# A float64-weight MLP pair behind attention: four conversion operations in two parts, low weights on VectorE, second activation read from its bank

## The chip, the cores and the metric

The kernel runs on one core of one Trainium2 chip. The metric is the device time of one launch in microseconds (us). Engines are named as in the profile: PE is TensorE (matmul), PEld its weight load, DVE is VectorE, ACT is ScalarE, POOL is GpSimd, SP is SyncE, which here only issues DMAs. [...]

## The reference, cut to what matters

```python
def _moe_ref(x, w_in, w_out):            # x 1792x768, w_in 768x2048, w_out 2048x768
    h = x @ w_in
    r = np.maximum(h, 0.0)
    g = r * r
    return (g @ w_out).astype(np.float32)

def _moe2_ref(x, w_in, w_out):
    h = x @ w_in
    relu6 = np.clip(h + 3.0, 0.0, 6.0)
    g = h * relu6 / 6.0
    return (g @ w_out).astype(np.float32)

def reference(**kwargs):
    ...
    attn_out = _attn_ref(**attn_kwargs)  # 4 batches, 12 heads, 448 rows, 64 per head
    ...
    x = _moe_ref(x=x, **moe_kwargs)
    return _moe2_ref(x=x, **moe2_kwargs)
```

The four weight matrices come as float64 (dividing a float32 array by a float64 scalar made them so); everything else is float32.

## The kernel before

Four batches are worked in two groups of two. Each group runs attention and then two MLPs. An MLP has a hidden phase (x @ w_in, then the activation) and a project phase (g @ w_out). Weights come in units of 128x768 numbers: 16 units for each phase, 64 for the two MLPs. A unit feeds 36 matmuls of 448 columns in two halves of 18, one for each batch of the group (e = 0 and 1). In the hidden phase each half sums in a PSUM bank of its own (two banks, tag `bm`), and its activation reads that bank.

Products are made exact enough by splitting: a number is rounded to fp32r (`wh`, `gh`, `xh`), and the remainder is kept beside it (`wl`, `gl`, `xl`); three products are summed. `split(n)` makes `wh` on ACT and `wl` from it; `act` is the activation; `split_g` makes `gh` (on DVE in the first MLP, on ACT in the second) and then `gl` on POOL.

Only group 0 reads the float64 weights: `load(n)` brings a unit as pairs of 32-bit words, `convert(n)` makes float32 of them with integer operations in place, and `store(n)` writes the float32 unit to DRAM, from where group 1 reads it back. So group 1 does the same matmuls with no conversion. All this lies in one tile `arena`: two slots for raw units, three (`wr`) for converted ones.

The order on each engine is the order in which the code is written (the scheduler is off), and each engine works its queue strictly in that order. `run` goes over the units. For unit n it writes: load a later unit; the activation of the second half of unit n-1 (`rest`); `convert(n + 2)`; `split(n + 1)`; `store(n)`; `split_g` of that `rest`; then the 18 matmuls of half 0, their activation and `split_g`, and the 18 matmuls of half 1. While group 0 projects for the second time, steps of group 1's attention stand between the units. At the start, `convert(0)`, `split(0)` and `convert(1)` stand among the last steps of the attention (`opening` and the main loop), beside `xr` copies out of PSUM (L314) and the splits of x.

Of the kernel before, what the change touches and what calls it, by code (L numbers as in the profile page):

```python
# [39 lines left out]

F64_LEAST = 2.0 ** -15
F64_MOST = (2.0 - 2.0 ** -3 - 2.0 ** -23 ) * 2.0 ** 16

# [15 lines left out]
def attention_mlp_kernel(ctx: ExitStack, tc, qT, kT, v, w_pre, w_post, mask, w1_in, w1_out, w2_in, w2_out, outT):  # L59
# [38 lines left out]
    w2f = cst.tile([R, G, RI], F32, name="w2f")  # L98
    three = cst.tile([P, 1], F32, name="three")

# [372 lines left out]
    class Mlps:  # L473
# [26 lines left out]

        def convert(self, n):

            if n >= len(self.units) or self.gi > 0:
                return
            words = self.raw(n).bitcast(U32).rearrange("p (n e) -> p n e", e=2)
            low, high = words[:, :, 0], words[:, :, 1]
            wr = self.wr(n)
            bits = wr.bitcast(U32)
            nc.scalar.activation(wr, high.bitcast(F32), AF.Abs)  # L509
            nc.vector.tensor_scalar(wr, wr, F64_LEAST, F64_MOST, op0=ALU.max, op1=ALU.min)  # L510
            nc.vector.tensor_scalar(  # L511
                bits, bits, 3, 0x7FFFFFFF, op0=ALU.logical_shift_left, op1=ALU.bitwise_and)
            nc.vector.tensor_scalar(  # L513
                high, high, 0x80000000, 0x40000000, op0=ALU.bitwise_and, op1=ALU.bitwise_or)
            nc.vector.scalar_tensor_tensor(  # L515
                out=bits, in0=low, scalar=29, in1=bits, op0=ALU.logical_shift_right, op1=ALU.bitwise_or)
            nc.vector.tensor_tensor(out=bits, in0=bits, in1=high, op=ALU.bitwise_xor)

# [5 lines left out]
        def split(self, n):  # L524
            if n >= len(self.units):
                return
            wh = sh.tile([P, self.W], F32R, tag="wh", name=f"wh{self.gi}_{n}", bufs=2)
            wl = sh.tile([P, self.W], F32R, tag="wl", name=f"wl{self.gi}_{n}", bufs=2)
            nc.scalar.activation(wh, self.wr(n), AF.Copy)  # L529
            nc.gpsimd.tensor_tensor(out=wl, in0=self.wr(n), in1=f(wh), op=ALU.subtract)  # L530
            self.ready[n] = wh, wl
# [12 lines left out]
        def act(self, which, fc, e, hp):  # L544
# [6 lines left out]
            else:  # L551
                a = sh.tile([P, S], F32, tag="w2", name=f"a{nm}", bufs=2)
                nc.scalar.activation(r, hp[:, :S], AF.Relu, bias=three)
                nc.scalar.activation(a, hp[:, :S], AF.Copy, scale=1.0 / 6.0)  # L554
                nc.vector.scalar_tensor_tensor(out=g, in0=r, scalar=6.0, in1=a, op0=ALU.min, op1=ALU.mult)
            return which, fc, e, g
# [58 lines left out]
        def run(self, mp, behind):  # L615

            rest = None
            for n, (kind, which, m, _) in enumerate(self.units):
                self.load(n + (3 if self.gi == 0 else 2))
                if rest:  # L620
                    rest = self.act(*rest)
                if n == 0:
                    self.split(1)
                self.convert(n + 2)
                if n > 0:
                    self.split(n + 1)
                self.store(n)
                if rest:
                    self.split_g(*rest)
                    rest = None  # L630
                wh, wl = self.ready.pop(n)
                if kind == "h":
# [14 lines left out]
                    hp = self.hidden(which, m, 0, wh, wl)  # L647
                    self.split_g(*self.act(which, m, 0, hp))
                    rest = (which, m, 1, self.hidden(which, m, 1, wh, wl))
# [31 lines left out]
    with tc.manual_schedule():  # L681
        nc.vector.memset(three, 3.0)
        warm = sh.tile([P, 1], F32, tag="wh", name="warm", bufs=2)
        nc.scalar.activation(warm, three, AF.Exp)
        att = Attention(0)
# [68 lines left out]
```

## Time and profile before

| | us |
|---|---|
| median of 3 runs | 1480.28 (1479.43 to 1483.08) |
| the profiled execution | 1481.33, of which its span is 1479.5 |
| PE busy | 1407.2 (95% of the span) |
| DVE, ACT, POOL busy | 754.5, 678.3, 718.3 (51%, 46%, 49%) |

The span runs from the first to the last instruction of the profiled execution; 1.83 us of its time lie outside. Shares are means over attention, hidden and project phases of both groups, which have different limits.

### The profile page before, as it was taken

To read this page: it belongs to the slowest core of one execution; us is meant where nothing else is said; L and a number is where in the kernel's file an instruction comes from. 1 tells how busy PE (TensorE), PEld (TensorE's weight loads), DVE (VectorE), ACT (ScalarE), POOL (GpSimd) and SP (SyncE) were. 2 spreads that over 40 slices of the span, in tenths; PEclk is the share of its full clock that TensorE was granted. 3 is DMA by queue.
4 is the path that set the end of the run, shared out by engine and by line. 5 is a ranking of instruction groups with operands and counts; after the bars stand their busy time and mean duration, and the time that the engine had idled before them with its cause. 6 is when DMAs were issued, how large, how long until landed. Compare 5 with 4: busy or idle time off the path is not lost.

```text
span 1479.5 us, 22801 instructions
## 1 busy us (share of the span) xinstructions
PE 1407.2 (95%) x8512; PEld 1253.7 (85%) x8512; DVE 754.5 (51%) x1356; ACT 678.3 (46%) x1293; POOL 718.3 (49%) x662
## 2 busy tenths in 40 slices
PE   8889999999999998889998999999999999999999
PEld 4678888788899987779997888889999999999998
DVE  4877667776777588888756786571110001111000
ACT  4767665444422344444436666664442113554121
POOL 1667766555532255443235677675554223555221
PEclk9999999999999999999999999999999999999999
DMA  5354533445465544447755444431111111111121
GB/s 143 108 142 112 147 102 99 149 131 158 131 198 152 160 129 128 128 128 210 213 176 145 127 119 142 116 103 54 54 54 54 54 54 54 54 54 54 54 91 49
DMA packets 72211, 167.53 MB, mean 113 GB/s; under 512 B 9125, under 2 KB 47525, under 8 KB 72101
## 3 DMA queue, kind: packets, MB, share of 16 engines
q1 hardware_dynamic: 68645, 160.59, 37.4%
q10 hardware_dynamic: 3456, 5.51, 1.0%
q8 instruction: 66, 1.08, 0.3%
q14 instruction: 44, 0.36, 0.1%
HBM read 96.86 MB, written 30.67 MB: 86 GB/s over the span
## 4 chain that ended last, share of the span: by engine, by line
PE 70%; DVE 16%; ACT 4%; issue 4%; POOL 4%; DMA 1%; SPq 0%; POOLq 0%; ACTq 0%; DVEq 0%
PE ps_a L587 21%; PE ps_h L573 16%; PE bs L587 9%; PE ps_o L279 8%; PE ps_x L306 5%; DVE arena L513 5%; DVE arena L515 3%; PE ps_m L231 2%; PE ps_m L233 2%; ACT arena L509 2%; PE bs L193 2%; PE bs L194 2%; PE ps_m L232 2%; DVE arena L510 1%; DVE arena L511 1%
## 5 line engine op out<-in xcount | busy, mean ns | idle before, releaser
L530 POOL TENSOR_TENSOR wl<-arena,wh 128x768 fp32r<-128x768 f32 x128 | 246.7, 1927 | 435.5 <-ACT wh L529 384.6
L224 POOL TENSOR_TENSOR tl<-t,th 120x448 fp32r<-120x448 f32 x165 | 192.5, 1167 | 36.7 <-ACT th L222 30.5
L529 ACT ACTIVATE wh<-arena 128x768 fp32r<-128x768 f32 x128 | 107.8, 842 | 218.7 <-PE bs L587 163.6
L587 PE MATMUL ps_a<-gh,wl 128*128 128x448 f32 x544 | 198.4, 365 | 2.5 <-POOL wl L530 2.5
L587 PE MATMUL ps_a<-gh,wh 128*128 128x448 f32 x544 | 199.4, 367 | 0.0
L279 PEld LDWEIGHTS ps_o<-w2s,p 120*112 120x112 f32 (+1 forms) x1440 | 174.1, 178 | 23.1 <-POOL w2s L268 13.3
L279 PE MATMUL ps_o<-w2s,p 120*112 120x120 f32 (+1 forms) x1440 | 180.6, 269 | 8.0 <-POOL w2s L268 8.0
L573 PE MATMUL ps_h<-yh,wh 128*128 128x448 f32 x384 | 141.7, 369 | 19.4 <-ACT a L554 19.4
L573 PE MATMUL ps_h<-xh,wl 128*128 128x448 f32 x384 | 141.8, 369 | 8.4 <-POOL wl L530 8.4
L573 PE MATMUL ps_h<-xl,wh 128*128 128x448 f32 x384 | 141.1, 367 | 0.9 <-DVE xl L541 0.6
L248 ACT ACTIVATE p<-ps_m,mx 120x448 f32<-120x448 f32 x180 | 113.2, 629 | 60.7 <-PE ps_o L279 28.8
L573 PE MATMUL ps_h<-xh,wh 128*128 128x448 f32 x384 | 140.6, 366 | 0.2 <-ACT r L549 0.2
L573 PE MATMUL ps_h<-yl,wh 128*128 128x448 f32 x384 | 140.7, 367 | 0.0
L573 PE MATMUL ps_h<-yh,wl 128*128 128x448 f32 x384 | 140.2, 365 | 0.0
L565 POOL TENSOR_TENSOR gl<-g,gh 128x448 fp32r<-128x448 f32 x80 | 95.9, 1204 | 78.8 <-ACT gh L564 44.3
L294 DVE COPY a<-ps_o 112x480 f32<-112x480 f32 (+1 forms) x176 | 114.4, 650 | 27.5 <-PE ps_o L279 26.4
L268 POOL TENSOR_SCALAR w2s<-w2f,rz 120x120 f32<-120x120 f32 x180 | 70.3, 390 | 118.7 <-DVE rz L260 102.3
L222 ACT ACTIVATE th<-t 120x448 fp32r<-120x448 f32 x180 | 102.6, 570 | 48.8 <-POOL tl L224 16.4
L587 PE MATMUL ps_a<-gl,wh 128*128 128x448 f32 x340 | 124.2, 365 | 0.0
L240 DVE TENSOR_REDUCE mx<-ps_m 120x1 f32<-120x448 f32 x180 | 109.2, 607 | 18.3 <-PE ps_m L233 18.3
L587 PEld LDWEIGHTS ps_a<-gh,wl 128*128 128x128 f32 x544 | 102.2, 188 | 11.8 <-POOL wl L530 3.6
L587 PEld LDWEIGHTS ps_a<-gh,wh 128*128 128x128 f32 x544 | 102.1, 188 | 8.3
(95 smaller groups left out, 2823.2 us busy)
## 6 DMA issues: line engine op xcount, KB each, us to landing
arena<-in_dram SPq DMA_DIRECT2D x64, 768.0 KB
t<-s SPq DMA_DIRECT2D x176, 210.0 KB
keep<-arena SPq DMA_DIRECT2D x64, 384.0 KB
arena<-keep SPq DMA_DIRECT2D x64, 384.0 KB
qr<-in_dram SPq DMA_DIRECT2D x60, 110.0 KB
v<-in_dram SPq DMA_DIRECT2D x12, 448.0 KB
outT_dram<-ot ACTq DMA_DIRECT2D x24, 224.0 KB
kr<-in_dram SPq DMA_DIRECT2D x18, 224.0 KB
```

What stands on the lines that cost most here:

```text
L222: nc.scalar.activation(th[:rows], tt[:rows], AF.Copy)
L224: eng.tensor_tensor(out=tl[:rows], in0=tt[:rows], in1=f(th[:rows]), op=ALU.subtract)
L240: nc.vector.reduce_max(mx[:rows], m[:rows, :S], axis=AX.X, negate=True)
L248: nc.scalar.activation(pt[:rows], m[:rows, :S], AF.Exp, bias=mx[:rows], accum_out=z[:rows])
L279: nc.tensor.matmul(o[:JP, q * G * ni:(q + 1) * G * ni], lhsT=pt[:rows, q * JP:(q + 1) * JP], rhs=w2s[:rows, :G * ni], start=True, stop=True)
L294: nc.vector.tensor_copy(dst, src)
L306: nc.tensor.matmul(xo[e * D:(e + 1) * D, k * n:(k + 1) * n], lhsT=self.v[:, q, g, :], rhs=self.aa[c][:, q, g, :n], start=(q == 0), stop=(q ...
L529: nc.scalar.activation(wh, self.wr(n), AF.Copy)
L530: nc.gpsimd.tensor_tensor(out=wl, in0=self.wr(n), in1=f(wh), op=ALU.subtract)
L565: nc.gpsimd.tensor_tensor(out=gl, in0=g, in1=f(gh), op=ALU.subtract)
L573: nc.tensor.matmul(hp[:, :S], lhsT=lw[:, c * P:(c + 1) * P], rhs=rw[:, c, cols], start=(k == 0), stop=(k == 3 * KC - 1))
L587: nc.tensor.matmul(acc[d, e][:, :S], lhsT=lw[:, wc], rhs=rw[fc, e], start=(fc == 0 and k == 0), stop=(fc == NF - 1 and k == 2))
```

## The change

`convert` gets four DVE operations in place of five, and two parts. ACT now scales the high words by 2^-112 (L510; it took their absolute value before). DVE clamps (L511), shifts left by 3 into the raw high words (L512), and joins that with the sign bit (L513: and, or); this is part 0. Part 1 is one operation that brings in the low words (L516). In a hidden unit part 1 is written behind the activation of half 0, in a project unit before the matmuls. `split(n + 1)` is written ahead of `convert(n + 2)`, and in group 0 its `wl` is made on DVE instead of POOL (L531). `store` runs one unit earlier. In both groups the second activation is one ACT and one DVE operation: the DVE operation takes h from the PSUM bank, and the ACT copy `a` is gone.

```diff
         def convert(self, n, part=None):
...
-            nc.scalar.activation(wr, high.bitcast(F32), AF.Abs)
-            nc.vector.tensor_scalar(wr, wr, F64_LEAST, F64_MOST, op0=ALU.max, op1=ALU.min)
-            nc.vector.tensor_scalar(
-                bits, bits, 3, 0x7FFFFFFF, op0=ALU.logical_shift_left, op1=ALU.bitwise_and)
-            nc.vector.tensor_scalar(
-                high, high, 0x80000000, 0x40000000, op0=ALU.bitwise_and, op1=ALU.bitwise_or)
-            nc.vector.scalar_tensor_tensor(
-                out=bits, in0=low, scalar=29, in1=bits, op0=ALU.logical_shift_right, op1=ALU.bitwise_or)
-            nc.vector.tensor_tensor(out=bits, in0=bits, in1=high, op=ALU.bitwise_xor)
+            if part != 1:
+                nc.scalar.activation(wr, high.bitcast(F32), AF.Copy, scale=F64_SCALE)
+                nc.vector.tensor_scalar(wr, wr, -F64_MOST, F64_MOST, op0=ALU.max, op1=ALU.min)
+                nc.vector.tensor_scalar(high, bits, 3, None, op0=ALU.logical_shift_left)
+                nc.vector.scalar_tensor_tensor(
+                    out=bits, in0=bits, scalar=0x80000000, in1=high, op0=ALU.bitwise_and, op1=ALU.bitwise_or)
+            if part != 0:
+                nc.vector.scalar_tensor_tensor(
+                    out=bits, in0=low, scalar=29, in1=bits, op0=ALU.logical_shift_right, op1=ALU.bitwise_or)
...
             nc.scalar.activation(wh, self.wr(n), AF.Copy)
-            nc.gpsimd.tensor_tensor(out=wl, in0=self.wr(n), in1=f(wh), op=ALU.subtract)
+            eng = nc.vector if self.gi == 0 else nc.gpsimd
+            eng.tensor_tensor(out=wl, in0=self.wr(n), in1=f(wh), op=ALU.subtract)
...
-                a = sh.tile([P, S], F32, tag="w2", name=f"a{nm}", bufs=2)
-                nc.scalar.activation(r, hp[:, :S], AF.Relu, bias=three)
-                nc.scalar.activation(a, hp[:, :S], AF.Copy, scale=1.0 / 6.0)
-                nc.vector.scalar_tensor_tensor(out=g, in0=r, scalar=6.0, in1=a, op0=ALU.min, op1=ALU.mult)
+                nc.scalar.activation(r, hp[:, :S], AF.Relu, bias=half, scale=1.0 / 6.0)
+                nc.vector.scalar_tensor_tensor(
+                    out=g, in0=r, scalar=1.0, in1=hp[:, :S], op0=ALU.min, op1=ALU.mult)
...
+                self.split(n + 1)
+                self.convert(n + 2, 0)
                 if n == 0:
-                    self.split(1)
-                self.convert(n + 2)
-                if n > 0:
-                    self.split(n + 1)
-                self.store(n)
+                    self.store(0)
+                self.store(n + 1)
                 if rest:
                     self.split_g(*rest)
                     rest = None
+                if kind == "p":
+                    self.convert(n + 2, 1)
...
-                    self.split_g(*self.act(which, m, 0, hp))
+                    done = self.act(which, m, 0, hp)
+                    self.convert(n + 2, 1)
+                    self.split_g(*done)
```

VectorE in group 0's first hidden phase, one unit. Before (L510 to L517 are a conversion, L562 makes `gh` for half 1 of one unit and half 0 of the next):

```order
L562 CAST gh_0_3_0_3407<-g_0_3_0_3656 128x448
L510 TENSOR_SCALAR arena_3255<-arena_3255 128x768
L511 TENSOR_SCALAR arena_3255<-arena_3255 128x768
L513 TENSOR_SCALAR arena_3255<-arena_3255 128x768
L515 SCALAR_TENSOR_TENSOR arena_3255<-arena_3255 128x768
L517 TENSOR_TENSOR arena_3255<-arena_3255 128x768
L562 CAST gh_0_3_1_3409<-g_0_3_1_3682 128x448
```

Now, one unit of the same phase on the same engine:

```order
L562 CAST gh_0_1_0_3397<-g_0_1_0_3527 128x448
L531 TENSOR_TENSOR wl_3_3558<-arena_3255,wh_3_3557 128x768
L511 TENSOR_SCALAR arena_3255<-arena_3255 128x768
L512 TENSOR_SCALAR arena_3255<-arena_3255 128x768
L513 SCALAR_TENSOR_TENSOR arena_3255<-arena_3255 128x768
L562 CAST gh_0_1_1_3399<-g_0_1_1_3554 128x448
L516 SCALAR_TENSOR_TENSOR arena_3255<-arena_3255 128x768
L562 CAST gh_0_2_0_3401<-g_0_2_0_3589 128x448
```

The low weights (L531) have come to the front, and the conversion's last operation (L516) now stands between the two `gh`.

VectorE in group 0's second hidden phase, one unit. Before (L555 makes g from `r` and `a`):

```order
L555 SCALAR_TENSOR_TENSOR g_1_3_1_5575<-r_1_3_1_5574,a_1_3_1_5576 128x448
L510 TENSOR_SCALAR arena_3255<-arena_3255 128x768
L511 TENSOR_SCALAR arena_3255<-arena_3255 128x768
L513 TENSOR_SCALAR arena_3255<-arena_3255 128x768
L515 SCALAR_TENSOR_TENSOR arena_3255<-arena_3255 128x768
L517 TENSOR_TENSOR arena_3255<-arena_3255 128x768
L555 SCALAR_TENSOR_TENSOR g_1_4_0_5614<-r_1_4_0_5613,a_1_4_0_5615 128x448
```

Now (L554 makes g from `r` and the PSUM bank `ps_h`):

```order
L554 SCALAR_TENSOR_TENSOR g_1_3_1_5525<-r_1_3_1_5524,ps_h_1_3_1_5504 128x448
L531 TENSOR_TENSOR wl_37_5529<-arena_3255,wh_37_5528 128x768
L511 TENSOR_SCALAR arena_3255<-arena_3255 128x768
L512 TENSOR_SCALAR arena_3255<-arena_3255 128x768
L513 SCALAR_TENSOR_TENSOR arena_3255<-arena_3255 128x768
L554 SCALAR_TENSOR_TENSOR g_1_4_0_5560<-r_1_4_0_5559,ps_h_1_4_0_5540 128x448
L516 SCALAR_TENSOR_TENSOR arena_3255<-arena_3255 128x768
```

Between g of half 1 and g of half 0 of the next unit there still stand four operations (five before); one conversion operation has moved behind that g.

VectorE where attention hands over to the first MLP. Before (L314 copies `ps_x`, attention's result, out of PSUM; the conversion is unit 0's):

```order
L314 COPY xr_688<-ps_x_6_2_3269 128x2x110
L510 TENSOR_SCALAR arena_3255<-arena_3255 128x768
L511 TENSOR_SCALAR arena_3255<-arena_3255 128x768
L513 TENSOR_SCALAR arena_3255<-arena_3255 128x768
L515 SCALAR_TENSOR_TENSOR arena_3255<-arena_3255 128x768
L517 TENSOR_TENSOR arena_3255<-arena_3255 128x768
L314 COPY xr_688<-ps_x_7_0_3305 128x2x118
```

Now:

```order
L314 COPY xr_688<-ps_x_6_2_3269 128x2x110
L511 TENSOR_SCALAR arena_3255<-arena_3255 128x768
L512 TENSOR_SCALAR arena_3255<-arena_3255 128x768
L513 SCALAR_TENSOR_TENSOR arena_3255<-arena_3255 128x768
L516 SCALAR_TENSOR_TENSOR arena_3255<-arena_3255 128x768
L531 TENSOR_TENSOR wl_0_3301<-arena_3255,wh_0_3300 128x768
L314 COPY xr_688<-ps_x_7_0_3304 128x2x118
```

The low weights of unit 0 stand between the conversion and the copy of `ps_x_7_0`.

## Rows read from the trace of the kernel before

**Rows 1.** Stages by windows, cut at their first matmuls: group 0's three, group 1's three.

```profile
core 0: us, PE busy (x) PEld busy (x) DVE busy (x) ACT busy (x) POOL busy (x), PEclk, DMA share, GB/s
261.61:393.93 132.32, 122.80 (x579) 106.85 (x577) 94.17 (x117) 59.99 (x100) 69.92 (x49) 1.00 0.50 147
393.93:513.20 119.27, 117.97 (x578) 107.88 (x576) 83.25 (x96) 33.51 (x45) 36.27 (x20) 1.00 0.57 169
513.20:653.53 140.33, 120.91 (x578) 107.07 (x577) 111.42 (x111) 71.07 (x126) 69.57 (x46) 1.00 0.42 127
1006.77:1123.98 117.21, 117.21 (x578) 108.26 (x577) 13.36 (x34) 47.62 (x80) 66.94 (x49) 1.00 0.18 55
1123.98:1241.53 117.55, 117.45 (x577) 108.04 (x576) 6.46 (x11) 19.90 (x28) 30.67 (x17) 1.00 0.18 54
1241.53:1358.66 117.13, 117.13 (x577) 108.15 (x576) 20.83 (x34) 63.95 (x111) 64.33 (x47) 1.00 0.18 54
```

**Rows 2.** Timeline, first hidden phase: start, length, engine, line, idle before and its releaser.

```profile
302.79 2.01 POOL L530 TENSOR_TENSOR wl<-arena,wh 128x768 fp32r<-128x768 f32 x1 [1.16 <-issue]
...
304.85 0.48 PE L573 MATMUL ps_h<-xh,wl 128*128 128x448 f32 x1 [0.62 <-POOL wl L530]
...
308.73 0.58 ACT L550 ACTIVATE g<-r 128x448 f32<-128x448 f32 x1 [4.12 <-POOL gl L565]
...
313.03 0.48 PE L573 MATMUL ps_h<-xh,wl 128*128 128x448 f32 x1 [0.58 <-POOL wl L530]
```

**Rows 3.** Timeline, second hidden phase.

```profile
561.25 2.21 DVE L513 TENSOR_SCALAR arena<-arena 128x768 uint32<-128x768 uint32 x1
...
566.84 0.58 ACT L564 ACTIVATE gh<-g 128x448 fp32r<-128x448 f32 x1 [4.54 <-DVE g L555]
...
568.43 0.48 PE L573 MATMUL ps_h<-yh,wh 128*128 128x448 f32 x1 [1.42 <-ACT a L554]
...
577.47 0.48 PE L573 MATMUL ps_h<-yh,wh 128*128 128x448 f32 x1 [1.44 <-ACT a L554]
```

**Rows 4.** All on tile `arena`: count, then minimum/median/maximum ns of one.

```profile
L529 ACT ACTIVATE wh<-arena x128: 827/846/859, 259.5 to 1461.4; 128x768 fp32r<-128x768 f32 x128
...
L509 ACT ACTIVATE arena<-arena x64: 876/898/927, 255.0 to 753.7; 128x768 f32<-128x768 f32 x64
L510 DVE TENSOR_SCALAR arena<-arena x64: 551/560/2104, 256.0 to 756.5; 128x768 f32<-128x768 f32 x64
...
L513 DVE TENSOR_SCALAR arena<-arena x64: 547/2196/2219, 257.1 to 759.9; 128x768 uint32<-128x768 uint32 x64
L515 DVE SCALAR_TENSOR_TENSOR arena<-arena x64: 943/948/2604, 257.5 to 760.4; 128x768 uint32<-128x768 uint32 x64
L517 DVE TENSOR_TENSOR arena<-arena x64: 957/958/2572, 258.5 to 761.4; 128x768 uint32<-128x768 uint32 x64
```

**Rows 5.** By line, 255 to 775 us: count, then minimum/median/maximum ns of one.

```profile
L562 DVE CAST gh<-g x32: 384/386/389, 276.2 to 405.2; 128x448 fp32r<-128x448 f32 x32
...
L565 POOL TENSOR_TENSOR gl<-g,gh x40: 1130/1233/1482, 276.7 to 608.2; 128x448 fp32r<-128x448 f32 x40
...
L597 DVE TENSOR_TENSOR yl<-ps_a,yh x8: 624/625/625, 449.0 to 512.8; 128x448 fp32r<-128x448 f32 x8
```

**Rows 6.** Groups by line, ACT, 530 to 645 us: busy us, mean ns of one.

```profile
L553 ACT ACTIVATE r<-ps_h,three 128x448 f32<-128x448 f32 x26 | 16.3, 626 | 0.0
```

**Rows 7.** Timeline at the hand-over from attention to the first MLP.

```profile
259.39 0.40 DVE L314 COPY xr<-ps_x 128x236 f32<-128x236 f32 x1
...
259.84 1.83 PE L306 MATMUL ps_x<-a,v 112*64 112x118 f32 x32 [1.20 <-DVE xr L314]
...
271.17 1.82 POOL L530 TENSOR_TENSOR wl<-arena,wh 128x768 fp32r<-128x768 f32 x1
...
273.04 0.47 PE L573 MATMUL ps_h<-xh,wl 128*128 128x448 f32 x1 [0.60 <-POOL wl L530]
```

More of the change, by code (lines that the diff above doesn't have):

```diff
@@ L37 @@
 }
-F64_LEAST = 2.0 ** -15
-F64_MOST = (2.0 - 2.0 ** -3 - 2.0 ** -23 ) * 2.0 ** 16
+F64_SCALE = 2.0 ** -112
+F64_MOST = (2.0 - 2.0 ** -3 - 2.0 ** -23) * 2.0 ** -96
 def chunks_of(seq):
@@ L98, in attention_mlp_kernel @@
     w2f = cst.tile([R, G, RI], F32, name="w2f")
-    three = cst.tile([P, 1], F32, name="three")
+    half = cst.tile([P, 1], F32, name="half")
     def load_constants():
@@ L499, in load, with convert @@
                 nc.sync.dma_start(out=self.wr(n), in_=kept[n])
-        def convert(self, n):
+        def convert(self, n, part=None):
             if n >= len(self.units) or self.gi > 0:
@@ L681, in attention_mlp_kernel @@
     with tc.manual_schedule():
-        nc.vector.memset(three, 3.0)
+        nc.vector.memset(half, 0.5)
         warm = sh.tile([P, 1], F32, tag="wh", name="warm", bufs=2)
-        nc.scalar.activation(warm, three, AF.Exp)
+        nc.scalar.activation(warm, half, AF.Exp)
         att = Attention(0)
```

## Prediction

> **What bounds the kernel now.** I read the stages by windows first, cut at the first matmul of each phase. Group 1 is the control: it does the same 576 matmuls a phase, with the weights already converted. Its phases take 117.21, 117.55 and 117.13 us with PE busy throughout, so 16 units cost 117.2 us and one unit 7.32. Group 0 takes 132.32 for its first hidden phase, 119.27 for the first project phase and 140.33 for the second hidden phase [rows 1]. The excess is 15.1, 1.7 and 23.2 us, 40.0 together. The granted clock is 1.00 in all six rows, the upper level, so none of it is clock. Outside these three stages the change reaches nothing that PE waits for.
>
> Next comes the timeline, to see which loop sets the pace. In the first hidden phase PE stops once a unit for `wl`, at 304.85 and again at 313.03, which is a period of 8.18 [rows 2]. Before that stop ACT had waited 4.12 us for a `gl` of POOL before it could make its next g (308.73, the same place of the next unit), because `gh`, and so `gl`, stands behind the whole conversion on DVE. The loop is g, ACT's conversion step, `wh`, `wl` on POOL, the end of the conversion, `gh`, `gl`, and the next g. In the second hidden phase the period is 577.47 - 568.43 = 9.04, and PE waits for ACT to free the bank of half 1 [rows 3]. ACT stands before `gh`, which waited 4.54 for g on DVE, and g is written behind the five conversion operations.
>
> In both loops one DVE operation is far off its price. L513 takes 0.55 at the least and 2.20 in the median [rows 4]; at 561.25 it took 2.21 [rows 3]. While POOL makes `wl` (2.01 in rows 2), DVE stands.
>
> **The change, part by part.** A unit must fit into 7.32 us in both loops.
>
> *Prices.* Clamp (L511) and shift (L512) are operations of one input like L510 and L513, 0.56 each; the shift writes every second word, as L513 did at 0.55. The two operations L513 and L516 have the form of L515: 0.95. `wl` on DVE is a difference of 768 numbers, nearest to L517: 0.96 [rows 4]. All five rows have maxima above 2.1, and that is the upper bound of each. ACT's scaled copy is priced as the absolute value, 0.90. For g with one input from PSUM the nearest row is L597, a DVE operation of 448 columns with one input from PSUM: 0.63 [rows 5]. The dropped ACT copy `a` is pure relief for ACT in both groups, and worth nothing in group 1, where PE never waits.
>
> *First hidden phase.* The new loop is: g 0.58 [rows 2], `wh` 0.85, `wl` 0.96, clamp 0.56, shift 0.56, join 0.95 [rows 4], `gh` 0.39, `gl` 1.23 [rows 5], together 6.08. ACT's scaled copy runs beside `wl` and costs nothing so; if `wl` did not cover it, it would be hidden only in part, and the loop would be longer by less than 0.1. The last operation L516 follows `gh` on DVE at once, while `gl` needs a hand-over to POOL, so L516 may get in first: 0.95 more, 7.03. Hand-overs between engines are small: `wl` ended at 304.80 and PE ran at 304.85 [rows 2]; three of them give 7.2. That is under 7.32, so PE should set the pace. `wl` now ends about 3 us into the unit before the one that needs it. A loop that is too long by 0.2 would thus use up this lead over a whole phase and not show.
>
> *Second hidden phase.* The new loop is: relu 0.63 [rows 6], `wh` 0.85, `wl` 0.96, clamp, shift and join 2.07, g of half 0 0.63, `gh` 0.58 [rows 3], then the next relu: 5.72. One `gl` falls among the clamp, shift and join and can hold DVE up for its length, 1.23: 6.95. This too is under 7.32. The bank of half 0 is now freed by DVE instead of ACT, behind the join. In a unit paced by PE this g ends near 5.7 to 6.3 of 7.32.
>
> *What is queued behind the new operations.* `wl` on DVE waits for PE to be done with the `wh`/`wl` buffers of two units ago. That is the start of the unit, and relu and `wh` on ACT come later anyway. In the project phases nothing else is on DVE but `wl`, the conversion and a few copies: 0.96 + 1.12 + 1.90 = 4.0 of 7.32. POOL keeps two `gl` per unit.
>
> *DMA.* A unit moves 768 KB in and 384 KB out, 1.18 MB. At 7.32 us that is 161 GB/s; the first project phase averages 169 [rows 1]. The raw slot is free once L516 is done, about 6 us into a unit, and is needed again some 10 us later. The store has a unit more of room than before. I take nothing for it.
>
> *The hand-over.* On DVE `wl` of unit 0 now stands ahead of the copy of `ps_x` that ran at 259.39. The conversion is shorter by about 0.5, then `wh` must be made (0.85) and `wl` (0.96), so the copy runs about 1.4 later. PE's last attention matmuls at 259.84 wait for it [rows 7], and the MLP starts 1.4 later, at 263.0. But its second unit was held until 273.04 by `wl` of unit 1, against 261.61 + 37 x 0.2034 = 269.1 at full pace. The chain to that `wl` gets shorter by one conversion operation (0.96) and by 1.82 - 0.96 = 0.86 for `wl` itself: 271.2; full pace from 263.0 gives 270.5. I take 271.0, a gain of 2.0. The bounds are 0.4 (the delay of 1.4 passes on whole) and 2.5.
>
> *The sum.* First hidden phase: 15.1 of excess, 3.9 of it at the hand-over. I gain 2.0 there and the other 11.2. The second hidden phase gives 23.2, and the project phase 1.0 of its 1.7 (its stop for the first `wl`). Together 37.4. The profiled execution took 1481.33 (span 1479.5), so 1443.9; the median of the runs is 1.05 below it, so **1443 us**. With its bounds (hand-over, project phase, 0.2 of pace in either phase) this case reaches from 1440 to 1449.
>
> **Rivals.**
>
> [...] The rows show that DVE and POOL hold each other up: L513 at 2.20 beside a POOL `wl` of 2.01. The change puts one more two-input operation on DVE. [...] Worked from rows: if both `gl` of a unit land in DVE's loop, the first phase has 7.03 + 1.23 = 8.26, no better than 8.18, and the second 5.72 + 2 x 1.23 = 8.18 against 9.04, a gain of 15 x 0.86 = 12.9. With 2.0 and 1.0 from the other places the gain is 15.9: about **1464**. [...]
>
> *DMA sets the pace.* If stage-wide traffic could not rise above the 147 GB/s of the first hidden phase, a unit would take 8.0, which costs 15 x 0.7 = 10.5 in the second hidden phase and as much in the first: about **1464** again. The 169 of the project phase speaks against it.
>
> *Slower.* If every two-input operation of 768 columns on DVE took its blocked price, 2.2, the first loop would be 0.58 + 0.85 + 3 x 2.2 + 1.12 + 0.39 + 1.23 = 10.8, or 2.6 over today's for 15 units; a project unit would need 3 x 2.2 + 1.12 = 7.7, or 0.4 over PE's pace for 32 units; the second phase would stay near 9. That is +39 + 13: about **1530**. It would decide from some 1.5 us for each of the three. Against it: L515 and L517 have medians at their minimum, and what blocked them was mostly the `wl` that leaves POOL.
>
> *No change.* PE's wait could pass to another wait of the same length: g of half 0 frees its bank behind join and clamp on DVE, and if that g came later than 7.32 into its unit in both phases the old periods could return. In the first phase no bank hangs on DVE, so only the second can lose: about **1466**, and no change at all would need both this and the second case: 1480.
>
> **How the numbers follow.** First case 0.70, second 0.13, DMA 0.04, the bank alone 0.04, no change 0.04, slower 0.05. A difference under 0.3% (4.4 us) can hardly be told from none in this kernel. Faster is the sum of the first four, 0.91; same 0.04; slower 0.05. The forecast is the first case. The range must reach partly into the second, whose times spread from 1449 to 1464: 1438 to 1462, the lower end being the whole 40.0 of excess (1440) with a little over for the second group's start.
>
> **What the new profile would show.** Right: both hidden phases of group 0 at 117 to 120 us cut at the same matmuls, the first one with some 3 us of stops in its first two units; no row of PE waiting for `wl` or for the second activation in steady units; L511 and L512 near 0.56, L513, L516 and `wl` near 0.95 in the median, `gl` longer than 1.23 in the first phase. Wrong: a hidden phase with a period above 7.4; medians above 1.2 for the DVE operations; PE waiting for g on DVE (L554); ACT's L510 waiting for a load in hidden phases. The forecast fails most easily if the two `gl` and DVE's five operations interleave badly, since the loops have 0.1 to 0.4 us to spare.

## The result and the profile after

The changed kernel takes **1443.15 us** in the median of 4 runs (1442.0 to 1447.1) against 1479.86 for the kernel before beside it (4 runs, 1476.05 to 1483.08). The ratio is 0.976, with a 95% interval of 0.973 to 0.979. The forecast was 1443.0. The profiled execution took 1442.0 us, with a span of 1440.2 (1479.5 before).

The page of the kernel after: busy time of each engine, and, in the second line, the shares of the chain that ended last.

```profile
PE 1397.0 (97%) x8512; PEld 1255.2 (87%) x8512; DVE 699.1 (49%) x1356; ACT 654.8 (45%) x1229; POOL 596.0 (41%) x598
...
PE 88%; DVE 4%; POOL 3%; issue 2%; DMA 2%; ACT 1%; SPq 0%; POOLq 0%; DVEq 0%; ACTq 0%
```

PE now holds 88% of that chain; it was 70%, with 16% for DVE. Where the time came from is read from the stages. These are the windows of the kernel after, group 0's three phases cut at the same matmuls as [rows 1] (length, busy us of PE, PEld, DVE, ACT and POOL, granted clock, DMA share, GB/s):

```profile
261.94:379.46 117.52, 117.49 (x579) 108.18 (x577) 89.95 (x118) 61.10 (x98) 46.89 (x33) 1.00 0.56 165
379.46:497.00 117.54, 117.44 (x577) 108.03 (x576) 68.56 (x92) 32.47 (x44) 2.95 (x3) 1.00 0.55 163
497.00:614.13 117.13, 117.13 (x577) 108.15 (x576) 93.21 (x114) 61.69 (x96) 35.73 (x31) 1.00 0.53 161
```

All three now have the length of group 1's phases (117.1 to 117.6), and PE has next to no idle time left in them. Against [rows 1] they are 14.8, 1.7 and 23.2 us shorter, 39.7 together. A later start of the first one takes 1.5 of that back (below), and the time up to the first conversion step happened to be 1.2 shorter in this execution; 39.7 - 1.5 + 1.2 = 39.4, and the span fell by 39.3. From the end of group 0's second hidden phase to the start of group 1's MLPs it is 353.29 us, and was 353.24.

The operations on the tile `arena` of the kernel after (count, minimum/median/maximum ns), which answer to [rows 4]:

```profile
L511 DVE TENSOR_SCALAR arena<-arena x64: 546/554/560, 254.8 to 718.1; 128x768 f32<-128x768 f32 x64
L512 DVE TENSOR_SCALAR arena<-arena x64: 560/562/1434, 255.4 to 718.7; 128x768 uint32<-128x768 uint32 x64
L513 DVE SCALAR_TENSOR_TENSOR arena<-arena x64: 957/959/962, 256.0 to 719.3; 128x768 uint32<-128x768 uint32 x64
L516 DVE SCALAR_TENSOR_TENSOR arena<-arena x64: 946/955/1815, 257.0 to 720.3; 128x768 uint32<-128x768 uint32 x64
L531 DVE TENSOR_TENSOR wl<-arena,wh x64: 948/958/1450, 258.8 to 725.2; 128x768 fp32r<-128x768 f32 x64
```

All medians are the forecast prices, 0.56 and 0.95, and the operation with a median of 2.20 is gone. But a median over all 64 units hides a stage. In the second hidden phase alone L512 is held in 15 of 16 units (497.0 to 614.1):

```profile
L512 DVE TENSOR_SCALAR arena<-arena x16: 561/1419/1434, 501.2 to 609.9; 128x768 uint32<-128x768 uint32 x16
```

In the first hidden phase 15 of 31 `gh` take about 1.35 for 0.39, one in each unit. So DVE and POOL go on holding each other up once a unit. Before it was more: L513 took 2.2 in nearly every unit of both hidden phases, and L515 1.9 in the second one.

First hidden phase, timeline of the kernel after (start, length, idle before and its releaser), the place of [rows 2]:

```profile
299.78 0.58 ACT L551 ACTIVATE g<-r 128x448 f32<-128x448 f32 x1
...
304.06 0.39 DVE L562 CAST gh<-g 128x448 fp32r<-128x448 f32 x1
...
304.37 0.95 DVE L516 SCALAR_TENSOR_TENSOR arena<-arena 128x768 uint32<-128x768 uint32 x1
...
304.60 1.73 POOL L565 TENSOR_TENSOR gl<-g,gh 128x448 fp32r<-128x448 f32 x1 [4.05 <-DVE gh L562]
...
305.23 1.35 DVE L562 CAST gh<-g 128x448 fp32r<-128x448 f32 x1
...
307.10 0.58 ACT L551 ACTIVATE g<-r 128x448 f32<-128x448 f32 x1
```

L516 gets in ahead of `gl`, as the forecast had it, and `gl` takes 1.73 instead of 1.2. But `gl` ends at 306.33, and the g that needs its buffer runs at 307.10 without a wait for it: the loop has 0.77 us to spare, where before ACT waited 4.12 at this place.

Second hidden phase, same view, the place of [rows 3]:

```profile
536.61 1.15 POOL L565 TENSOR_TENSOR gl<-g,gh 128x448 fp32r<-128x448 f32 x1 [2.36 <-ACT gh L564]
...
536.74 1.43 DVE L512 TENSOR_SCALAR arena<-arena 128x768 uint32<-128x768 uint32 x1
...
539.09 0.61 DVE L554 SCALAR_TENSOR_TENSOR g<-r,ps_h 128x448 f32<-128x448 f32 x1
...
541.19 0.64 ACT L553 ACTIVATE r<-ps_h,half 128x448 f32<-128x448 f32 x1 [0.88 <-PE ps_h L573]
```

One `gl` in each unit falls on the shift and holds it up (1.43 for 0.56). g from PSUM comes on time all the same, and the last row has the direction of the wait turned round: ACT waits 0.88 for PE, where PE waited 1.4 for ACT.

The hand-over from attention, same view, which answers to [rows 7]:

```profile
258.85 0.96 DVE L531 TENSOR_TENSOR wl<-arena,wh 128x768 fp32r<-128x768 f32 x1 [0.91 <-ACT wh L529]
259.73 0.40 DVE L314 COPY xr<-ps_x 128x236 f32<-128x236 f32 x1
...
260.18 1.83 PE L306 MATMUL ps_x<-a,v 112*64 112x118 f32 x32 [2.71 <-DVE xr L314]
```

The copy L314 stands behind `wl`, and PE waits 2.71 for it (1.20 before). Counted from the start of ACT's first conversion step, the MLP starts after 8.08 us and not 6.57, that is 1.5 later. In exchange the phase then runs without the stops of its first units. In this execution the granted clock stayed at 1.00 after the wait; in e2, e3 and e5, with a wait of 2.70 to 2.73, it fell to 0.50 (last section).

The 1.7 us of the project phase were two stops of PE for POOL's `wl` in the kernel before, in the phase's first two units; both are gone:

```profile
394.84 0.47 PE L587 MATMUL ps_a<-gh,wl 128*128 128x448 f32 x1 [0.58 <-POOL wl L530]
...
403.01 0.47 PE L587 MATMUL ps_a<-gh,wl 128*128 128x448 f32 x1 [0.61 <-POOL wl L530]
```

### The profile page after: what moved, and what is told of

Read it like the earlier page. It is cut to its first block, busy times and chain, and to the rows that moved or that the text cites. A ratio compares the mean times of both kernels' runs of the same rounds, so it can differ in the third digit from the quotient of the medians.

```text
span 1440.2 us, 22752 instructions
## 1 busy us (share of the span) xinstructions
PE 1397.0 (97%) x8512; PEld 1255.2 (87%) x8512; DVE 699.1 (49%) x1356; ACT 654.8 (45%) x1229; POOL 596.0 (41%) x598
## 4 chain that ended last, share of the span: by engine, by line
PE 88%; DVE 4%; POOL 3%; issue 2%; DMA 2%; ACT 1%; SPq 0%; POOLq 0%; DVEq 0%; ACTq 0%
PE ps_h L573 33%; PE ps_a L587 22%; PE bs L587 9%; PE ps_o L279 8%; PE ps_x L306 5%; PE ps_m L231 2%; PE ps_m L233 2%; PE ps_m L232 2%; PE bs L193 2%; PE bs L194 2%; DVE khl L156 2%; POOL tl L224 1%; DMA t<-s 1%; PE ps_s L355 1%; DVE mx L240 1%
## 5 line engine op out<-in xcount | busy, mean ns | idle before, releaser
L531 POOL TENSOR_TENSOR wl<-arena,wh 128x768 fp32r<-128x768 f32 x64 | 118.3, 1849 | 242.7 <-ACT wh L529 239.5
```

The costliest lines, as they stand in the source:

```text
L531: eng.tensor_tensor(out=wl, in0=self.wr(n), in1=f(wh), op=ALU.subtract)
```

## Experiments

**How they are read.** The time before group 0's MLPs varies by several us between the profiled executions, though attention's code is the same in all (ACT's first conversion step starts between 249.2 and 255.8 us). From the end of group 0's second hidden phase to group 1's MLPs it is 353.1 to 358.3. So variants that differ by less than about 0.3% are told apart by stages. Each row of this table is taken from the starts of matmuls in one profiled execution: the length of group 0's three phases, and the time from the start of ACT's first conversion step to the first matmul of the project phase and to the end of the second hidden phase.

| kernel | hidden 1 | project | hidden 2 | conversion to project | conversion to end | median us | ratio (95%) |
|---|---|---|---|---|---|---|---|
| before | 132.3 | 119.3 | 140.3 | 138.9 | 398.5 | | 1 |
| after | 117.5 | 117.5 | 117.1 | 125.6 | 360.3 | 1443.2 | 0.976 (0.973 to 0.979) |
| e1_wl_pool | 122.4 | 117.9 | 117.1 | 128.7 | 363.7 | 1445.2 | 0.976 (0.974 to 0.978) |
| e2_one_part | 117.8 | 117.5 | 117.5 | 126.9 | 361.9 | 1445.9 | 0.976 (0.973 to 0.978) |
| e3_copy_back | 118.3 | 117.5 | 117.1 | 126.9 | 361.5 | 1444.7 | 0.975 (0.972 to 0.978) |
| e4_five_ops | 117.8 | 117.5 | 122.2 | 127.2 | 367.0 | 1447.6 | 0.977 (0.975 to 0.979) |
| e5_convert_first | 117.7 | 117.6 | 117.1 | 126.9 | 361.6 | 1445.9 | 0.978 (0.976 to 0.980) |
| e6_only_wl | 119.3 | 117.7 | 129.9 | 128.9 | 376.5 | 1463.6 | 0.990 (0.988 to 0.992) |
| e7_only_act | 132.2 | 119.3 | 136.2 | 138.8 | 394.4 | 1475.8 | 0.997 (0.995 to 0.998) |
| e8_only_conv | 125.6 | 118.4 | 131.6 | 131.9 | 381.9 | 1463.4 | 0.989 (0.987 to 0.991) |
| e9_wl0_pool | 119.9 | 117.5 | 117.1 | 126.2 | 360.8 | 1443.2 | 0.975 (0.973 to 0.976) |
| e10_order_only | 132.9 | 119.8 | 139.4 | 139.4 | 398.6 | 1481.2 | 1.000 (0.999 to 1.001) |
| e11_one_more | 120.1 | 117.7 | 117.3 | 130.3 | 365.4 | 1444.4 | 0.976 (0.974 to 0.978) |
| e12_two_more | 134.6 | 125.4 | 133.1 | 146.2 | 404.7 | 1487.6 | 1.005 (1.003 to 1.006) |

One part of the table is no effect of an edit. Up to the project phase e3 is the same program as the changed kernel, and it takes 1.3 us longer, because the granted clock fell to 0.50 for 3.4 us at the hand-over (last section). It fell there in e2, e3, e4, e5, e6, e11 and e12 and in no other row, so some 1.3 us in "conversion to project" and "conversion to end" say nothing.

The theory is the prediction's: each phase runs at the longest of PE's pace (7.32 us a unit) and its two loops. The rivals were that the new order made the gain, that POOL's `wl` alone was the cause, that the count of DVE operations alone was, and that ACT's copy `a` held the bank.

### One edit undone

**e1_wl_pool**: `wl` of group 0 back on POOL.

```diff
-            eng = nc.vector if self.gi == 0 else nc.gpsimd
+            eng = nc.gpsimd
```

> The changed kernel with group 0's wl made on POOL again, all else as changed. Theory (each hidden unit is paced by a loop over ACT, DVE and POOL, and the change brought both loops under PE's 7.32 us): wl on POOL takes 1.85 to 2.0 us and holds DVE's clamp, shift and join up meanwhile. First loop 0.58 + 0.85 + 2.0 + 2.08 + 0.39 + 0.95 + 1.23 = 8.1, second 0.63 + 0.85 + 2.0 + 2.08 + 0.63 + 0.58 = 6.8, 8.0 with one gl. First hidden phase 120 to 128 us in place of 117.5, second 117 to 126; time 1446 to 1460. Rival (the shorter conversion and activation alone suffice, the place of wl does not matter): both phases 117 to 118, time as the changed kernel within 0.3%.

The whole time hardly moves: 1445.2 is under the 1446 to 1460 expected, and what the rival had. The first hidden phase does: 122.4. Its timeline, one unit:

```profile
302.69 0.58 ACT L551 ACTIVATE g<-r 128x448 f32<-128x448 f32 x1 [3.17 <-POOL gl L565]
...
304.13 1.86 POOL L531 TENSOR_TENSOR wl<-arena,wh 128x768 fp32r<-128x768 f32 x1
...
304.83 1.58 DVE L511 TENSOR_SCALAR arena<-arena 128x768 f32<-128x768 f32 x1 [1.92 <-ACT arena L510]
...
310.21 0.58 ACT L551 ACTIVATE g<-r 128x448 f32<-128x448 f32 x1 [3.37 <-POOL gl L565]
```

The blocking is back: POOL's `wl` stretches the clamp from 0.55 to 1.58. From g to g it is 7.52 us, so this loop is 0.2 longer than PE's pace. The expected 8.1 added up `wl` and the clamp, which run beside each other here (304.13 to 305.99 and 304.83 to 306.41). PE's matmul rows show no stop for it in steady units. A matmul row is 0.37 long, but the next one starts 0.20 after it, so that a short stop leaves little or no gap between two rows. The weight loads show it:

```profile
321.07 0.19 PEld L573 LDWEIGHTS ps_h<-xh,wl 128*128 128x128 f32 x1 [0.30 <-POOL wl L531]
328.60 0.19 PEld L573 LDWEIGHTS ps_h<-xh,wl 128*128 128x128 f32 x1 [0.31 <-POOL wl L531]
```

These two are of nine such rows, one a unit from 313.56 on. The first units after the hand-over had none: there the lead of `wl` over the matmul that needs it was being used up, from 1.13 us in the third unit to 0.11 in the eighth, 0.2 in each, as the prediction said of a loop that is too long by 0.2. The nine units together are 1.6 us too long. The rest of the 4.9 by which the phase is longer, 3.3, lies in its first two units, and 1.9 of it comes back at the hand-over, since the MLP starts earlier when `wl` does not stand ahead of L314. In the second hidden phase the place of `wl` is worth nothing as long as the other edits stand.

**e2_one_part**: the conversion in one piece, where part 0 stood.

```diff
-                self.convert(n + 2, 0)
+                self.convert(n + 2)
...
-                    self.convert(n + 2, 1)
```

> The changed kernel with the conversion in one piece: the last operation (low words) stands right behind the join. Theory: first loop stays at 7.0, since that operation came ahead of gl anyway: 117.5. Second loop 5.72 + 0.95 = 6.67, with one gl 7.9: 117 to 123. Time within 0.4% of the changed kernel. Rival (the two parts are what made it): a loss of over 10 us in the second phase.

From the first conversion to the end it is 1.6 us longer, of which 1.3 are the clock at the hand-over. What the split into two parts is worth are the 0.4 of the second hidden phase, and nothing that a whole time shows. The first loop takes the 0.95 of the last operation ahead of `gh`, and `gl` is no longer held for it (1.16 in the median). In the second it uses up the room: a few units take up to 7.43.

**e3_copy_back**: the ACT copy `a` again, g made from it.

```diff
+                a = sh.tile([P, S], F32, tag="w2", name=f"a{nm}", bufs=2)
-                nc.vector.scalar_tensor_tensor(
-                    out=g, in0=r, scalar=1.0, in1=hp[:, :S], op0=ALU.min, op1=ALU.mult)
+                nc.scalar.activation(a, hp[:, :S], AF.Copy)
+                nc.vector.scalar_tensor_tensor(out=g, in0=r, scalar=1.0, in1=a, op0=ALU.min, op1=ALU.mult)
```

> The changed kernel with the second activation through an ACT copy of h again (bank freed by ACT, g from two SBUF inputs). Theory: second loop 0.54 longer, 6.3, with one gl 7.5, and g may now be held up by gl: second hidden phase 117 to 122, first unchanged. Time within 0.4% of the changed kernel. Rival (reading the bank is what made the second phase faster): second hidden phase above 128.

The second hidden phase stays at 117.1 with the copy. In the full set this edit is worth nothing there. The g made from `a` (L556) took 0.62 at 536.09, 538.95 and 543.41, so no hold by `gl` shows in it. The 0.8 by which the first phase is longer is the clock at the hand-over, which this edit doesn't reach.

**e4_five_ops**: the old five operations in one piece at part 0's place, with the other edits kept.

```diff
+            if part == 1:
+                return
...
+            nc.vector.tensor_scalar(
+                high, high, 0x80000000, 0x40000000, op0=ALU.bitwise_and, op1=ALU.bitwise_or)
...
+            nc.vector.tensor_tensor(out=bits, in0=bits, in1=high, op=ALU.bitwise_xor)
```

> The changed kernel with the old five-operation conversion in one piece at the place of part 0. Theory: both loops 1.52 longer than with part 0 alone: first 7.6 without the last operation behind gh, covered by the lead of wl, 117.5 to 122; second 7.24, with one gl 8.5: 122 to 132. Time 1447 to 1462. Rival (the number of operations does not matter once wl is off POOL): both phases 117 to 118, no loss.

Of the undone edits this one costs most: the second hidden phase goes to 122.2. Its timeline, ACT:

```profile
566.27 0.58 ACT L566 ACTIVATE gh<-g 128x448 fp32r<-128x448 f32 x1 [2.97 <-DVE g L556]
...
573.92 0.58 ACT L566 ACTIVATE gh<-g 128x448 fp32r<-128x448 f32 x1 [2.97 <-DVE g L556]
```

The period is 7.65, 0.33 over PE's pace; 15 units by 0.33 are 5.0, and the phase is 5.1 longer. Here the bank itself is what PE waits for, and it has no lead. The expectation had 7.24 for this loop, or 8.5 with one `gl` in it; one `gl` is in it, and holds L513 up by 0.87 in 15 of 16 units.

**e5_convert_first**: part 0 written ahead of the split again (`self.split(n + 1)` behind `self.convert(n + 2, 0)`, as before the change).

> The changed kernel with part 0 of the conversion written ahead of the split again (the order of before). Theory: the loops hardly change: first 0.58 + 0.90 + 2.08 + 0.96 + 0.39 + 0.95 + 1.23 = 7.1, second 0.63 + 0.90 + 2.08 + 0.96 + 0.63 + 0.58 = 5.8, with one gl 7.0. Both phases 117 to 118.5; time within 0.3% of the changed kernel. Rival (the order is what all four variants that kept the gain have in common, and it makes the gain): first phase above 122, second above 125.

Both hidden phases stay at PE's pace. The order is not needed. (The 1.3 us more up to the project phase are the clock at the hand-over.)

**e9_wl0_pool**: `wl` of unit 0 alone on POOL, to take it from ahead of L314.

```diff
-            eng = nc.vector if self.gi == 0 else nc.gpsimd
+            eng = nc.vector if self.gi == 0 and n > 0 else nc.gpsimd
```

> The changed kernel with wl of unit 0 alone on POOL, so that the copy of attention's result does not stand behind it on DVE. Theory: PE's last attention matmuls wait 0.9 in place of 2.7 for that copy and the MLP starts 1.8 earlier against the end of attention; what is left at the hand-over are the splits of x, so from ACT's first conversion step to the first project matmul 124 to 125.6 us in place of 125.6. The whole time cannot show it (under 0.3%). Rival (the delayed start is hidden by what comes after): 125.6 and no change.

PE's wait for L314 falls from 2.71 to 0.84, and the MLP starts 1.9 us earlier. It is lost again: the phase is 2.4 longer, with stops of PE for `wl`, `xl` and `r` in its first units. From the first conversion to the project phase it is 126.2 against 125.6, just outside the expected 124 to 125.6, and the whole time is that of the changed kernel (1443.2). So the later start that I priced is real, but hides stops that would come otherwise. Against the executions whose clock fell at the hand-over (126.9 in e2, e3 and e5) e9 is 0.7 ahead; how often it falls in the changed kernel is not shown, since one execution of each kernel was profiled.

### One edit alone on the kernel before

**e6_only_wl** (`wl` of group 0 on DVE), **e7_only_act** (the new second activation), **e8_only_conv** (four operations, in one piece) and **e10_order_only** (`split(n + 1)` ahead of `convert(n + 2)`):

```diff
-            nc.gpsimd.tensor_tensor(out=wl, in0=self.wr(n), in1=f(wh), op=ALU.subtract)
+            eng = nc.vector if self.gi == 0 else nc.gpsimd
+            eng.tensor_tensor(out=wl, in0=self.wr(n), in1=f(wh), op=ALU.subtract)
```

> The kernel before with group 0's wl on DVE, nothing else changed. Theory: first loop 0.58 + 0.90 + 3.59 + 0.96 + 0.39 + 1.23 = 7.65, and wl comes last, so there is no lead: first phase 121 to 126. Second 0.63 + 0.54 + 0.90 + 3.59 + 0.96 + 0.63 + 0.58 = 7.8, with one gl 9.06: 124 to 142. Time 1450 to 1478. Rival (POOL's wl alone was the trouble): both phases 117 to 119, time 1443.

> The kernel before with the second activation read from the bank, nothing else changed. Theory: first phase 132 as before; second loop 9.04 less the copy of 0.54: 8.5, second phase 130 to 136. Time 1470 to 1476. Rival (the copy was what held the bank and with it PE): second phase 117 to 119, time 1457.

> The kernel before with the four-operation conversion in one piece at the old place, nothing else changed. Theory: the loops still have wl on POOL and the conversion ahead of the split; what falls away is clamp or shift, of which one stood blocked anyway. First loop about 7.8, first phase 124 to 129; second loop 7.7 to 8.9, second phase 122 to 138. Time 1455 to 1472. Rival (the operation count alone): both phases 117 to 119, time 1443.

> The kernel before with split written ahead of the conversion, nothing else changed (five operations, wl on POOL, copy a). Theory: first loop 0.58 + 0.85 + 2.0 + 3.59 + 0.39 + 1.23 = 8.1 to 8.6, of which the lead of wl covers 4 us once: 125 to 133; second 0.63 + 0.54 + 0.85 + 2.0 + 3.59 + 0.63 + 0.58 = 8.8: 130 to 140. Time 1465 to 1480. Rival (the order is what made the gain): both phases under 122, time under 1450.

From the first conversion to the end of the second hidden phase the four gain 22.0, 4.1, 16.6 and 0. That is 42.7 together, and the whole change gains 38.2. Three expectations were missed by a little: e6's first hidden phase (121 to 126 us expected), e7's second (130 to 136) and e10's time (1465 to 1480). No single edit is enough, as the second hidden phase shows. In e6 PE waits for `wl` at a period of 8.26:

```profile
565.45 0.47 PE L574 MATMUL ps_h<-yh,wl 128*128 128x448 f32 x1 [0.66 <-DVE wl L531]
...
573.71 0.47 PE L574 MATMUL ps_h<-yh,wl 128*128 128x448 f32 x1 [0.67 <-DVE wl L531]
```

In e7 the wait for the bank is only handed from ACT's copy to DVE's g, 570.09 - 561.49 = 8.60:

```profile
561.49 0.47 PE L572 MATMUL ps_h<-yh,wh 128*128 128x448 f32 x1 [0.99 <-DVE g L553]
...
570.09 0.47 PE L572 MATMUL ps_h<-yh,wh 128*128 128x448 f32 x1 [1.01 <-DVE g L553]
```

In e8 a POOL `wl` still lies on the conversion and one of its operations takes 2.49 (period 572.07 - 563.63 = 8.44):

```profile
563.63 0.47 PE L573 MATMUL ps_h<-yh,wh 128*128 128x448 f32 x1 [0.85 <-ACT a L554]
...
565.60 2.49 DVE L513 SCALAR_TENSOR_TENSOR arena<-arena 128x768 uint32<-128x768 uint32 x1
...
572.07 0.47 PE L573 MATMUL ps_h<-yh,wh 128*128 128x448 f32 x1 [0.85 <-ACT a L554]
```

e10 leaves both hidden phases within 1 us of the kernel before. This refutes the order as the cause; e6 refutes POOL's `wl` alone; e8 refutes the count of operations alone; e7 refutes the copy, which passed a wait on that began with g on DVE.

### More work in the loop

**e11_one_more** and **e12_two_more** write the join (L513) two and three times, to the same values: 0.96 us of DVE more per unit, and 1.92. They ask how near the changed kernel is to its edge.

```diff
                 nc.vector.scalar_tensor_tensor(
                     out=bits, in0=bits, scalar=0x80000000, in1=high, op0=ALU.bitwise_and, op1=ALU.bitwise_or)
+                nc.vector.scalar_tensor_tensor(
+                    out=bits, in0=bits, scalar=0x80000000, in1=high, op0=ALU.bitwise_and, op1=ALU.bitwise_or)
```

> The changed kernel with the join operation done twice (same result). Theory: in its profile the loops have 0.8 to 0.9 us to spare a unit, and wl a lead of some 4 us over a phase; one more operation of 0.96 gives loops of 7.4 to 7.6, covered by the lead: both phases 117 to 119, time as the changed kernel. Rival (DVE and POOL collide, each further operation costs its time): both phases 125 or more.

> The changed kernel with the join operation done three times (same result). Theory: loops of 8.3 to 8.6, (8.4 - 7.32) x 15 = 16 less the lead of 4: both phases 126 to 134, time 1462 to 1476. In the project phases DVE has 4.0 + 1.9 = 5.9 of 7.32, no loss. Rival (DVE, half idle over the span, has room): both phases 117 to 119, time as the changed kernel.

With one more the whole time is 1444.4, inside the runs of the changed kernel. By stages it costs 5.1 us: 2.2 of a later MLP start (1.0 is the added operation, 1.2 the clock at the hand-over) and 2.5 in the first hidden phase, whose loop is now 7.57. At 120.1 that phase is above the expected 117 to 119: its second to sixth unit still take 7.32 to 7.34, then the lead is used up. PE again shows it in its weight loads alone, 0.35 to 0.39 in nine units; two of them:

```profile
317.63 0.19 PEld L575 LDWEIGHTS ps_h<-xh,wh 128*128 128x128 f32 x1 [0.39 <-ACT r L552]
325.21 0.19 PEld L575 LDWEIGHTS ps_h<-xh,wh 128*128 128x128 f32 x1 [0.36 <-ACT r L552]
```

With two more it is 1487.6, slower than the kernel before and far above the expected 1462 to 1476. The first hidden phase goes at 8.57 us a unit:

```profile
332.04 0.58 ACT L555 ACTIVATE g<-r 128x448 f32<-128x448 f32 x1 [4.92 <-POOL gl L569]
...
334.62 0.48 PE L577 MATMUL ps_h<-xh,wh 128*128 128x448 f32 x1 [0.97 <-ACT r L554]
...
340.61 0.58 ACT L555 ACTIVATE g<-r 128x448 f32<-128x448 f32 x1 [4.93 <-POOL gl L569]
```

The step from 7.57 to 8.57 is the added operation, now in full, and the second hidden phase follows at 8.31. That is the theory's edge: below PE's pace an operation of 0.96 is nearly free (e11's second hidden phase takes 117.3 us against 117.1), above it it costs its length in each of 32 hidden units (30.3 us more than e11 in the two hidden phases). DVE's busy share tells nothing of that edge: in e11 DVE still idles for a sixth of the first hidden phase (100.1 busy of 120.1), and the loop has already passed PE's pace. Even so the two hidden phases take 267.7 us together, less than the 272.6 of the kernel before. What puts e12 behind it is outside them: the MLP starts 11.65 after the first conversion step (6.57 before), and the project phase lost 7.8 us against the changed kernel. For that phase the expectation had no loss, since DVE has work for only 5.9 of each 7.32; the last section has what it left out.

## Why the prediction was right

**What bounds.** The 40 us of excess in group 0's stages were the gain that could be had, and 38.2 of it came, counted from the first conversion to the end of the second hidden phase. Nothing changed outside. The clock had no part in it: 1.00 in the three stages before and after. The lower value that these traces show, 0.50, stands in the kernel before in attention, from 26.50 to 29.50 us.

**Prices.** Clamp and shift 0.554 and 0.562 (forecast 0.56), join, L516 and `wl` 0.959, 0.955 and 0.958 (0.95 and 0.96), ACT's scaled copy 0.89 (0.90), g from PSUM 0.62 (0.63). The nearest rows held for operations that the kernel before did not have. One reading did not hold: the prediction took one DVE operation in each loop for held up, and relied on a median of L515 that is near its minimum. That median is over all 64 units. In the second hidden phase of the kernel before (513.2 to 653.5) it reads:

```profile
L515 DVE SCALAR_TENSOR_TENSOR arena<-arena x15: 943/1905/1912, 519.2 to 644.7; 128x768 uint32<-128x768 uint32 x15
```

At 563.37 it took 1.91 beside a `gl` of 1.48 that had begun at 562.99, so what held it was not the `wl` that the change takes off POOL. So the argument against the slower case, that POOL's `wl` did most of the blocking, is weaker than it reads there. In the changed kernel a `gl` still holds an operation in each unit, for 0.86 where the forecast allowed 1.23 for one.

**First hidden phase and hand-over.** Forecast 13.2 for both. From the first conversion to the first project matmul it is 138.85 before and 125.60 after, so 13.25. The later start is 1.5 (forecast 1.4). The net gain at the hand-over is the 14.8 of the phase less the 11.2 of its steady units and less 1.5: 2.1, against 2.0. That agreement is in part luck: the forecast has no term for the clock, and in e3, the same program up to the project phase, its fall costs 1.3 of the 2.1. One sentence of the forecast does not fit its own sum: it spoke of some 3 us of stops in the first two units, while its working left 0.5 (271.0 against 270.5). In the profile the first two units are 0.4 us over PE's pace, and the only wait for another engine in this phase is 0.4 of a weight load for ACT.

**The loops.** The first was worked out at about 7.2. What is measured is 7.32 - 0.77 = 6.55, and e11 gives the same: 7.57 - 0.96 = 6.61. The estimate was 0.6 too long. It added all of L516's 0.95 to `gl`, and the row of `gl` grew by 0.6 (1.73 for 1.15), since it starts while L516 is under way. And rows that follow each other overlap a little: from g to `gh` it is 304.06 - 299.78 = 4.28, and the sum of durations was 4.46. The direction was safe: a loop that is shorter still is hidden by PE. For the second loop one row gives the room, ACT's wait of 0.88 for PE, so about 7.32 - 0.88 = 6.4 against the 6.95 of the forecast (e11 puts 0.96 more into it and its later units stay at 7.32, so the room may be a little more).

**Second hidden phase.** All of the 23.2 came. L512 held up by one `gl` was the case forecast.

**Project phase.** 1.7 came against 1.0: the whole excess of the phase [rows 1], both of its stops for `wl`. I had counted one of them.

**Sum.** 37.4 forecast, 38.2 measured. The medians of the runs stand 36.7 apart and the profiled executions 39.3. Of the latter 1.2 is time before the first conversion step; why the medians stand closer is not shown, since one execution of each kernel was profiled. That the median came within 0.2 us of the forecast is luck: the runs of the changed kernel reach from 1442.0 to 1447.1, and a sum that was 0.8 short met medians that stand 36.7 apart and not 38.2.

**The rivals.** *The second case*, both `gl` of a unit in DVE's loop: DVE and POOL do hold each other up still, once a unit: L512 at 1.42 in the second hidden phase, `gh` at 1.35 and `gl` at 1.73 in the first. Part of it lies in the loops (L512, `gl`), but both loops end before PE needs them. What lets two operations hold each other up is not shown. L512, which has one input, was held by a `gl` that had begun 0.13 earlier (536.74 and 536.61). The g from PSUM (L554) took 0.611 to 0.624 in all its 64 rows, but none of them ran beside a POOL operation for more than 0.02; the g of the kernel before (L555), from `r` and `a`, took 0.617 to 0.659. No row shows that g from PSUM is less exposed. What decided was whether a held operation is on the path. *DMA*: 161 to 165 GB/s in the hidden phases, more than the 147 that this rival had as the ceiling. *The bank alone* and *no change* are refuted for the whole change, but e7 and e4 show that the mechanism exists: undo enough of the rest, and the bank is waited for again, from DVE. *Slower*: the three two-input operations did not take 2.2 (medians 0.955 to 0.959). It took some two us more of DVE work in each unit to get behind the kernel before (e12), and not by its hidden phases.

**What stays open.** How the gain divides among the edits has no single answer, since they overlap: 42.7 in sum when each is done alone, but 14.3 in sum when each of e1 to e5 is undone (3.4, 1.6, 1.3, 6.7 and 1.3 against the table's 360.3), and some 9 of that without the clock at the hand-over. Whether `wl` on DVE and four operations alone would do, with none of the other edits, was not run. The earlier `store` was not undone either; in the kernel before, ACT's conversion step waited for a store ten times (37.2 us), all in the project phase, where PE did not stop for it, and never in a hidden phase. A kernel faster than the changed one did not come out of this: the three phases stand at PE's pace, and e9, the only try at the hand-over, gained nothing in the whole time.

## What to carry to other kernels

Write each loop between engines as a sum of rows and set it against the pace of the engine that should bound; the longest one counts, and an operation in a loop below that pace is nearly free (117.3 us against 117.1 in e11's second hidden phase), while the same operation above it costs its length in every unit (e12 against e11: 0.96 us a unit more, and 30.3 us in the two hidden phases). Edits that shorten the same loop do not add up, so test each alone and each undone before saying which one made the gain. Take the median of an operation by stage: over the whole kernel it can hide that nearly every one in a stage was held (L512: 0.562 over all, 1.419 in the second hidden phase). A matmul row here is 0.37 us long and the next starts 0.20 after it, and the stops of e1, e4 and e11 (0.16 to 0.45, all but the first one of e4) stood in the rows of the weight loads only, so look there before calling a stage free of waits.

## What the runs showed of the hardware that was not expected

In e12 the project phase took 125.4 us where the loops allow 117.5. At 466.18 PE had stood 3.31 us for a `yl` that DVE makes behind the lengthened conversion, and the granted clock fell. The row of that matmul, and then windows of the same kernel (length, PE busy, granted clock, DMA share, GB/s):

```profile
466.18 0.74 PE L591 MATMUL ps_a<-gh,wh 128*128 128x448 f32 x1 [3.31 <-DVE yl L601]
```

```profile
450.00:458.00 8.00, 8.00 (x41) 1.00 0.49 156
458.00:466.00 8.00, 4.87 (x24) 0.93 0.52 147
...
466.20:471.50 5.30, 5.30 (x14) 0.50 0.73 223
471.60:474.00 2.40, 2.40 (x13) 0.98 0.00 0
474.00:482.00 8.00, 8.00 (x42) 1.00 0.52 147
```

For 5.3 us after the stop the granted clock is 0.50, and 14 matmuls start there where 26 would at the pace of 0.2034 us each; that is 2.4 us on top of the stop. The three other stops of the project phase (0.53, 0.23 and 0.53), the 3.31 and the 2.4 make 7.0 of the 7.8 lost; the rest is that a matmul row shows each of the four stops some 0.2 short. The stops of about 1.0 us in the first hidden phase of the same kernel, one a unit, left the clock at 1.00 (270.40 to 401.90).

The same was seen at the hand-over, and the longer wait there came with the change. Where PE waited 0.84 to 1.20 for L314 (the kernel before, e1, e7, e8, e9, e10), the granted clock stayed at 1.00. Of the eight profiled executions in which it waited 2.70 or more, it fell to 0.50 in seven, for 3.4 us (6.8 in e12). The changed kernel is the one in which it did not, at 2.71; e2, e3 and e5 had 2.70 to 2.73. The row of e3, and then windows 1.3 us after PE went on, of e3 and of the changed kernel:

```profile
255.51 2.26 PE L306 MATMUL ps_x<-a,v 112*64 112x118 f32 x32 [2.72 <-DVE xr L314]
...
256.80:260.10 3.30, 3.30 (x18) 0.50 0.02 9
...
261.47:264.77 3.30, 3.30 (x26) 1.00 0.05 20
```

Up to the project phase the two kernels are the same program, and e3 takes 126.9 where the changed kernel takes 125.6.

The shift L512, which writes every second word, runs as fast as the contiguous clamp (0.562 against 0.554). The stops of 0.2 to 0.45 us per unit that matmul rows do not show were new to me: in e4 they made one phase 5.1 us longer, and in all units but the first the only PE row that names them is that of the weight load.
